# Token mixing steps drawn from one queue in a fused attention, mixture and gated-convolution kernel

## The chip, the cores and the metric

The kernel runs on one core of one Trainium2 chip. The metric is the device time of one execution in microseconds (us), as the median of several runs. The core has five engines that matter here: PE (TensorE, matrix products), DVE (VectorE), ACT (ScalarE), POOL (GpSimd) and SP (SyncE, which issues the DMAs). Each works through its own list of instructions in order and waits for the others only through semaphores.

## What is computed

Batch 4, sequence 768, 8 heads of 48, so 384 channels. The reference, cut to what matters:

```python
# gated linear attention, per batch and head
state = alpha[t][:, None] * state + outer(k[t], v[t]);  x[t] = q[t] @ state
# mixture
theta = x @ w_theta
zr, zi = x * cos(theta), x * sin(theta)
y = w_tok_r @ zr + w_tok_i @ zi        # over the sequence: token mixing
u = x + y
x = u + relu(u @ w_ch)
# gated convolution
h = relu(x @ w_in);  out = (h * sigmoid(conv3(h, conv_w))) @ w_out
```

## The kernel before

The sequence of each batch is cut into six chunks of 128 rows. Chunks are numbered through: 0 to 5 are batch 0, 6 to 11 batch 1, 12 to 17 batch 2, 18 to 23 batch 3. All float32 products are made of three matmuls of split operands (`mm3`, L66: high by high, high by low, low by high), so a value is first split into a rounded high part (ACT, L72) and a rest (DVE, L73).

Three kinds of step are given in program order by the loops at L400 to L423:

- `a_att(b, c)` (L376): attention of one chunk. It loads the chunk after next, prepares the next one on DVE (`a_prep`: two scans L229 and L234 over the decays with a reciprocal L233 between, and a product L243 that scales q and k), makes the next chunk's scores on PE (`kps`, `sc`), and then computes the chunk's own `y` (scores by v, then q by the running state S), copies it to `x`, computes `kv` for the state, and transposes x (`xps`) into `u`. The new state is `tst` on DVE (L296, old S plus `kv`), then two products by the decay on POOL (L304).
- `a_theta(ci)` (L325): splits u (`zh`, L72 and L73), nine matmuls `th`, then sine and cosine on ACT with DVE between (L343 to L347, tile `zf`, two buffers), the product with x (L348), and the split into `zh` and `zl` (six buffers each). L344 on DVE is the last reader of the `th` bank.
- `m_mix(b, h, c)` (L355): token mixing, chunk c's share of half h (384 of 768 output rows) of batch b: 18 matmuls `yps` into three accumulators of the pool `ps_m`, which has three buffers. After the sixth chunk three DVE additions (L374) move them into `u`. Four batches, two halves and six chunks make 48 steps and 864 matmuls.

The token weights come as 64-bit words: `load_tok` loads a piece, DVE decodes it in three instructions (L115 to L117), and the returned function, called as `piece()` one step later, splits it into `wtok`. Six pieces belong to the first half, six to the second.

Before the change, batch 0's six attention steps run with its theta steps one behind and no mixing. Then, for each batch b, mixing of its first half goes with the attention of batch b + 1, and mixing of its second half with the theta steps of batch b + 1. The last batch is mixed behind the loop, where the weights of the later layers are loaded (L429 to L440): its first half at L441, its second half at L475 with the first channel products (`cps`) between. The rest (`hps` and `ops`, L580 on) follows.

PSUM has eight banks: three for `ps_m`, five for `ps_a`, which `kps`, `sc`, `y`, `kv`, `xps` and `th` share in turn. A tile of `ps_a` therefore waits until the fifth tile before it, in program order, has been read.

The program order is not the order on the engines. The framework schedules the instructions of each engine itself when the kernel is built (an instruction may pass earlier ones that are not ready by its own estimate of the times), so a matmul written later can stand earlier on PE.

Of the kernel before, what the change touches and what calls it, by code (L numbers as in the profile page):

```python
# [19 lines left out]
B, H, S, D = 4, 8, 768, 48  # L20
# [3 lines left out]
NC = S // P  # L24
# [20 lines left out]
def tile_gated_linear_attention__then__spectral_moe__then__conv_gate(  # L45
# [53 lines left out]
    def body(top, slow):  # L99
# [46 lines left out]
        with ExitStack() as ph1:  # L146
# [244 lines left out]
            if not slow:  # L391
                a_load(0)
                a_load(1)
                wps = ps_a.tile([P, 512], F32, tag="a", name="wps")
                ohf = onehot.rearrange("p a t -> p (a t)")
                for _ in range(NWARM):
                    nc.tensor.matmul(wps, ohf[:, :P], ohf[:, :512], start=True, stop=True)
                a_prep(0)
                a_score(0)
            for c in range(NC):  # L400
                a_att(0, c)
                if c == 0:
                    load_theta()
                else:
                    piece()
                piece = load_tok(0, c)
                if c > 0:
                    a_theta(c - 1)
            piece()
            a_theta(NC - 1)  # L410
            for b in range(B - 1):
                for c in range(NC):
                    m_mix(b, 0, c)
                    a_att(b + 1, c)
                    if b == 0:
                        if c > 0:
                            piece()
                        piece = load_tok(1, c)
                if b == 0:
                    piece()  # L420
                for c in range(NC):
                    m_mix(b, 1, c)
                    a_theta((b + 1) * NC + c)  # L423
            marks.clear()
            att_ctx.close()
            ps_n = top.enter_context(tc.tile_pool(name="ps_n", bufs=5, space=PSUM))
# [11 lines left out]
            cst = st_p.tile([P, 9 * 256], F32, tag="w", name="cst", bufs=STB)  # L438
            nc.sync.dma_start(out=cst[:, : 6 * NF].bitcast(U32), in_=conv_w.rearrange("p f k -> p (f k)").bitcast(U32))
            decode(cw.rearrange("p f k -> p (f k)"), cst, 3 * NF)  # L440
            for c in range(NC):  # L441
                m_mix(B - 1, 0, c)
            tok0_ctx.close()
            ux_p = top.enter_context(tc.tile_pool(name="ux", bufs=2, side="right"))

# [27 lines left out]
                xsp[b, h] = x2  # L473

            for c in range(NC):  # L475
                m_mix(B - 1, 1, c)
                if c == 1:
                    m_usplit(0, 0)
                    m_ch(0, 0, ps_n, "n")
                if c == 2:  # L480
                    m_usplit(0, 1)
                    m_ch(0, 1, ps_n, "n")
                if c == 3:
                    m_xsplit(0, 0)
# [211 lines left out]
```

## Time and profile before

| | |
|---|---|
| median of 3 runs | 580.08 us (578.15 to 581.35) |
| profiled execution | 579.94 us, of which the span from first to last instruction is 578.2 us |
| mean granted clock of TensorE | 0.978 of full speed |
| busy shares of the span | PE 96%, DVE 79%, ACT 59%, POOL 16% |
| token mixing matmuls `yps` | 864 of 4407 matmuls; 23% of the chain that ended last |
| DMA | 65.41 MB, 113 GB/s in the mean |

A busy share is a mean over the whole span; the stages differ. PE counts as busy while a matmul is in its pipeline, so a full PE can still run at half clock. Times within the profile count from the first instruction of the span.

### The profile page before, as it was taken

Reading aid. Unit: us, or ns where it says so; the run is one execution under the profiler, and the core shown is the slowest. Engines: PE = TensorE matmul, PEld = TensorE weight load, DVE = VectorE, ACT = ScalarE, POOL = GpSimd, SP = SyncE. Lnnn points to the kernel's source line nnn. Section 1 sums busy time; section 2 is a strip of 40 time slices with the busy share of each in tenths; the row PEclk is TensorE's granted clock in tenths of the full one; section 3 lists DMA queues with packets and bytes.
Section 4 is the critical chain, followed back from the end, with each engine's and each line's share of the span. In section 5 each row is a group of like instructions: output and inputs, shape, how many; then the busy total and the mean of one; then the engine's idle time right before and its main releaser. Section 6 shows DMA issues by size and latency. Waiting matters only on the chain.

```text
span 578.2 us, 10973 instructions
## 1 busy us (share of the span) xinstructions
PE 553.1 (96%) x4407; PEld 532.9 (92%) x4407; DVE 457.1 (79%) x688; ACT 338.4 (59%) x695; POOL 93.6 (16%) x99
## 2 busy tenths in 40 slices
PE   6878989989999999999999999999999999999995
PEld 3767879979999999999999999999999999999995
DVE  7899997899856676542658889997888889798780
ACT  3665655555864567542752345567776776667561
POOL 2447514341044400350000000000000000000000
PEclk9688998999999999999999999999999999999999
DMA  8454652564024500320014333401044544546001
GB/s 322 153 170 136 212 187 81 174 220 161 1 83 139 174 20 8 97 64 1 1 31 160 111 112 109 145 20 41 5 147 139 176 137 144 198 143 204 27 29 46
DMA packets 24986, 65.41 MB, mean 113 GB/s; under 512 B 2528, under 2 KB 8672, under 8 KB 24544
## 3 DMA queue, kind: packets, MB, share of 16 engines
q1 hardware_dynamic: 24928, 64.64, 33.9%
q8 instruction: 36, 0.59, 0.4%
q14 instruction: 22, 0.18, 0.1%
HBM read 59.92 MB, written 4.72 MB: 112 GB/s over the span
## 4 chain that ended last, share of the span: by engine, by line
PE 80%; DVE 3%; issue 1%; ACT 1%; ACTq 0%
PE yps L64 23%; PE hps L64 18%; PE ops L64 18%; PE cps L64 7%; PE th L64 5%; PE y L64 4%; PE sc L64 3%; PE kv L64 2%; PE xps L320 1%; PE kps L252 1%; DVE fbt L229 1%; DVE stage L116 1%; DVE fbt L234 0%; DVE wtok L73 0%; DVE stage L115 0%
## 5 line engine op out<-in xcount | busy, mean ns | idle before, releaser
L64 PE MATMUL yps<-wtok,zh 128*128 128x384 f32 x576 | 153.0, 343 | 0.0
L64 PEld LDWEIGHTS yps<-wtok,zh 128*128 128x128 f32 x576 | 105.2, 191 | 2.4 <-ACT pt L261 0.2
L64 PE MATMUL hps<-x,win 128*128 128x386 f32 x576 | 107.1, 339 | 0.0
L64 PE MATMUL ops<-wout,g 128*128 128x384 f32 x576 | 106.9, 338 | 0.0
L64 PEld LDWEIGHTS hps<-x,win 128*128 128x128 f32 x576 | 102.2, 189 | 0.0
L64 PEld LDWEIGHTS ops<-wout,g 128*128 128x128 f32 x576 | 101.7, 187 | 0.0
L64 PE MATMUL yps<-wtok,zl 128*128 128x384 f32 x288 | 96.9, 339 | 0.0
L262 POOL TENSOR_SCALAR_AFFINE_SELECT pt<-pt 128x512 f32<-128x512 f32 x48 | 53.8, 1142 | 147.6 <-ACT pt L261 147.6
L64 PEld LDWEIGHTS yps<-wtok,zl 128*128 128x128 f32 x288 | 54.4, 189 | 0.8
L521 ACT ACTIVATE cv<-cv 128x384 f32<-128x384 f32 x64 | 33.4, 523 | 32.1 <-DVE cv L518 32.1
L229 DVE TENSOR_TENSOR_SCAN fbt<-a_t,onehot 128x516 f32<-128x516 f32 x24 | 29.5, 1229 | 22.9 <-ACT a_t L240 21.2
L73 DVE TENSOR_TENSOR g<-cv,g 128x384 fp32r<-128x384 f32 x64 | 35.5, 555 | 14.8 <-ACT g L72 14.2
L64 PE MATMUL th<-wth,zh 128*128 128x384 f32 x216 | 44.0, 340 | 0.0
L515 DVE SCALAR_TENSOR_TENSOR cv<-hh,cw,cv 128x383 f32<-128x383 f32 (+1 forms) x64 | 38.3, 613 | 4.4 <-ACT cv L512 4.1
L522 DVE SCALAR_TENSOR_TENSOR cv<-cv,hh 128x384 f32<-128x384 f32 x64 | 35.2, 556 | 7.9 <-ACT cv L521 5.9
L512 ACT ACTIVATE cv<-hh,cw 128x384 f32<-128x384 f32 x64 | 38.3, 616 | 3.8 <-DVE g L73 3.3
L64 PE MATMUL cps<-us,wch 128*128 128x384 f32 x216 | 40.3, 339 | 0.0
L72 ACT CAST g<-cv 128x384 fp32r<-128x384 f32 x64 | 32.6, 509 | 11.6 <-DVE cv L522 10.1
L518 DVE SCALAR_TENSOR_TENSOR cv<-hh,cw,cv 128x384 f32<-128x384 f32 (+1 forms) x64 | 38.4, 614 | 0.7
L64 PEld LDWEIGHTS cps<-us,wch 128*128 128x128 f32 x216 | 38.0, 188 | 0.5 <-issue 0.3
L64 PEld LDWEIGHTS th<-wth,zh 128*128 128x128 f32 x216 | 37.4, 188 | 0.5 <-DVE zh L73 0.4
L64 PE MATMUL sc<-qk_t 48*128 48x128 f32 x384 | 34.3, 294 | 3.1 <-DVE tst L296 2.5
(84 smaller groups left out, 826.8 us busy)
## 6 DMA issues: line engine op xcount, KB each, us to landing
qk_t<-in_qka_dram SPq DMA_DIRECT2D x24, 512.0 KB, 4.6
stage<-in_w_tok_dram SPq DMA_DIRECT2D x12, 768.0 KB, 4.5
top<-in_w_tok_dram SPq DMA_DIRECT2D x12, 768.0 KB, 4.3
a_t<-in_qka_dram SPq DMA_DIRECT2D x24, 260.0 KB, 2.8
v_t<-in_v_dram SPq DMA_DIRECT2D x24, 192.0 KB, 3.9
out_dram<-ob SPq DMA_DIRECT2D x24, 192.0 KB, 1.9
stage<-in_w_in_dram SPq DMA_DIRECT2D x4, 768.0 KB, 5.8
stage<-in_w_out_dram SPq DMA_DIRECT2D x4, 768.0 KB, 4.4
```

Source lines behind the costliest of these rows:

```text
L64: nc.tensor.matmul(o, lhsT, rhs, start=start, stop=stop, skip_group_check=True)
L72: cast = nc.scalar.copy(hi, src)
L73: lo_eng.tensor_tensor(lo, src, hi.bitcast(F32), ALU.subtract)
L116: nc.vector.scalar_tensor_tensor(fb, hi, 0xC0000000, fb, ALU.bitwise_and, ALU.bitwise_or)
L229: nc.vector.tensor_tensor_scan(bf[:, AW:0:-1], at[:, AW:0:-1], of[:, AW:0:-1], 0.0, ALU.mult, ALU.add)
L252: nc.tensor.transpose(kps[:, p, :], kh[:, p, :], ident)
L262: nc.gpsimd.affine_select(pt, pt, [[0, NP], [1, P]], ALU.is_ge, 0.0, base=0, channel_multiplier=-1)
L512: nc.scalar.activation(cv, hh[:, o : o + HALF], AF.Copy, scale=cw[:, f, 1:2])
L515: nc.vector.scalar_tensor_tensor(cv[:, a:HALF], hh[:, o + a - 1 : o + HALF - 1], cw[:, f, 0:1], cv[:, a:HALF], ALU.mult, ALU.add)
L518: nc.vector.scalar_tensor_tensor(cv[:, 0:e], hh[:, o + 1 : o + 1 + e], cw[:, f, 2:3], cv[:, 0:e], ALU.mult, ALU.add)
L521: nc.scalar.activation(cv, cv, AF.Tanh, scale=0.5)
L522: nc.vector.scalar_tensor_tensor(cv, cv, 1.0, hh[:, o : o + HALF], ALU.add, ALU.mult)
```

## The change

The 48 mixing steps are put in one list (`mixes`), ordered by batch, half and chunk, and the loops take the next one with each step of attention or theta, from chunk 2 of batch 0 on. So batch 0's first half starts two chunks behind its theta steps, its last two shares go with the first two chunks of batch 1, and its second half follows at once. By the end of the loops 40 steps have been taken where it was 36; eight are left for the place behind the loop instead of twelve. The theta steps of batches 1 to 3 now go with the last two shares of the batch before and the first four shares of their own batch. `a_theta(5)`, the last of batch 0, moves behind the first attention step of batch 1, and the loads and splits of the second half's weights move one step.

```diff
--- before.py
+++ after.py
@@ -397,6 +397,7 @@
                     nc.tensor.matmul(wps, ohf[:, :P], ohf[:, :512], start=True, stop=True)
                 a_prep(0)
                 a_score(0)
+            mixes = [(b, h, c) for b in range(B) for h in range(2) for c in range(NC)]
             for c in range(NC):
                 a_att(0, c)
                 if c == 0:
@@ -404,23 +405,24 @@
                 else:
                     piece()
                 piece = load_tok(0, c)
+                if c > 1:
+                    m_mix(*mixes.pop(0))
                 if c > 0:
                     a_theta(c - 1)
-            piece()
-            a_theta(NC - 1)
-            for b in range(B - 1):
+            for b in range(1, B):
                 for c in range(NC):
-                    m_mix(b, 0, c)
-                    a_att(b + 1, c)
-                    if b == 0:
-                        if c > 0:
-                            piece()
+                    if b == 1:
+                        piece()
                         piece = load_tok(1, c)
-                if b == 0:
-                    piece()
+                    m_mix(*mixes.pop(0))
+                    a_att(b, c)
+                    if b == 1 and c == 0:
+                        a_theta(NC - 1)
                 for c in range(NC):
-                    m_mix(b, 1, c)
-                    a_theta((b + 1) * NC + c)
+                    if b == 1 and c == 0:
+                        piece()
+                    m_mix(*mixes.pop(0))
+                    a_theta(b * NC + c)
             marks.clear()
             att_ctx.close()
             ps_n = top.enter_context(tc.tile_pool(name="ps_n", bufs=5, space=PSUM))
@@ -438,8 +440,8 @@
             cst = st_p.tile([P, 9 * 256], F32, tag="w", name="cst", bufs=STB)
             nc.sync.dma_start(out=cst[:, : 6 * NF].bitcast(U32), in_=conv_w.rearrange("p f k -> p (f k)").bitcast(U32))
             decode(cw.rearrange("p f k -> p (f k)"), cst, 3 * NF)
-            for c in range(NC):
-                m_mix(B - 1, 0, c)
+            while mixes[0][1] == 0:
+                m_mix(*mixes.pop(0))
             tok0_ctx.close()
             ux_p = top.enter_context(tc.tile_pool(name="ux", bufs=2, side="right"))
 
@@ -473,7 +475,7 @@
                 xsp[b, h] = x2
 
             for c in range(NC):
-                m_mix(B - 1, 1, c)
+                m_mix(*mixes.pop(0))
                 if c == 1:
                     m_usplit(0, 0)
                     m_ch(0, 0, ps_n, "n")
```

What the engines' lists look like at the places that matter. In the names a number tells the tile apart; `wtok00` and `wtok01` are high and low part of the first half's weights, `wtok10` and `wtok11` of the second's.

PE, at `kv` of chunk 6, the first chunk of batch 1 (`x_920` and `x_974` are its x). Before:

```order
L64 MATMUL y_903<-v_t_620,pt_750 64x48 x2
L64 MATMUL y_903<-v_t_620,pt_753 64x48 x2
L64 MATMUL y_903<-v_t_620,pt_750 64x48 x2
L64 MATMUL y_903<-v_t_620,pt_753 64x48 x2
L64 MATMUL kv_922<-v_t_620,kt_756 64x96 x8
L64 MATMUL yps_845<-wtok00_84,zh_797 128x384
L64 MATMUL yps_845<-wtok01_85,zh_797 128x384
L64 MATMUL yps_846<-wtok00_84,zh_797 128x384
L64 MATMUL yps_846<-wtok01_85,zh_797 128x384
L64 MATMUL yps_847<-wtok00_84,zh_797 128x384
L64 MATMUL yps_847<-wtok01_85,zh_797 128x384
L320 MATMUL xps_936<-ident_73,x_920 128x128 x3
```

With the change:

```order
L64 MATMUL y_957<-v_t_659,pt_807 64x48 x2
L64 MATMUL y_957<-v_t_659,pt_810 64x48 x2
L64 MATMUL y_957<-v_t_659,pt_807 64x48 x2
L64 MATMUL y_957<-v_t_659,pt_810 64x48 x2
L64 MATMUL kv_976<-v_t_659,kt_813 64x96 x8
L320 MATMUL xps_990<-ident_73,x_974 128x128 x3
L64 MATMUL th_998<-wth0_115,zh_995 128x384
L64 MATMUL th_998<-wth1_116,zh_995 128x384
L64 MATMUL th_998<-wth0_115,zh_995 128x384 x2
L64 MATMUL th_998<-wth1_116,zh_995 128x384
L64 MATMUL th_998<-wth0_115,zh_995 128x384 x2
L64 MATMUL th_998<-wth1_116,zh_995 128x384
```

Six token matmuls stood between `kv` and the transposes; now the transposes follow at once, and behind them the nine matmuls of theta step 5 (`th_998`), which before (`th_825`) stood ahead of this chunk's `y`. The fifth `ps_a` tile before this `kv` was the `th` of theta step 5 and is now that of theta step 4. Counted over PE's list, 72 token matmuls stand ahead of the first `y` of batch 1 in both programs; ahead of the `y` of chunk 11, the last of batch 1, there are 156 before and 180 with the change. Between the last theta matmul and the first `cps` there are 126 before and 102 with the change.

DVE, around the `tst` behind `kv` of chunk 9, from which POOL makes the state for chunk 10. Before:

```order
L243 TENSOR_TENSOR qk_t_1180<-qk_t_1180,fbt_1291 128x1024
L296 TENSOR_TENSOR tst_1251<-S1_112,kv_1242 112x384
L115 TENSOR_SCALAR stage_1262<-stage_1262 128x768
L73 TENSOR_TENSOR zh_1487<-u_935,zh_1487 128x384
L116 SCALAR_TENSOR_TENSOR stage_1262<-stage_1262 128x768
L117 SCALAR_TENSOR_TENSOR stage_1262<-stage_1262 128x768
L73 TENSOR_TENSOR wtok11_87<-stage_1155,wtok10_86 128x2x384
L229 SCALAR_TENSOR_TENSOR fbt_1394<-a_t_1285,onehot_109 128x516
L233 RECIPROCAL starts_110<-fbt_1394 128x4
```

With the change:

```order
L116 SCALAR_TENSOR_TENSOR stage_1347<-stage_1347 128x768
L296 TENSOR_TENSOR tst_1336<-S1_112,kv_1327 112x384
L117 SCALAR_TENSOR_TENSOR stage_1347<-stage_1347 128x768
L73 TENSOR_TENSOR wtok11_87<-stage_1240,wtok10_86 128x2x384
L229 SCALAR_TENSOR_TENSOR fbt_1476<-a_t_1370,onehot_109 128x516
L73 TENSOR_TENSOR zh_1647<-u_989,zh_1647 128x384
L233 RECIPROCAL starts_110<-fbt_1476 128x4
L234 SCALAR_TENSOR_TENSOR fbt_1476<-a_t_1370,starts_110 128x516
L243 TENSOR_TENSOR qk_t_1372<-qk_t_1372,fbt_1476 128x1024
```

Before, the one-input decode step L115 stands behind `tst`; now L117, the split of a token weight piece and the next scan do, and `zh` comes behind the scan. From the start of DVE's list to the L243 for the scores of chunk 12, the changed list has one more L115, L116, L117 and `wtok` split and two more `zh` splits, and nothing less.

PE in the theta steps of batch 2 (chunks 12 to 17; `th_2403` is that of chunk 14 before, `th_2481` with the change). Before:

```order
L64 MATMUL yps_2299<-wtok11_87,zh_1610 128x384
L64 MATMUL yps_2299<-wtok10_86,zl_1630 128x384
L64 MATMUL th_2403<-wth0_115,zh_2400 128x384
L64 MATMUL th_2403<-wth1_116,zh_2400 128x384
L64 MATMUL yps_2297<-wtok10_86,zh_1651 128x384
L64 MATMUL yps_2297<-wtok11_87,zh_1651 128x384
L64 MATMUL yps_2297<-wtok10_86,zl_1671 128x384
L64 MATMUL yps_2297<-wtok10_86,zh_1651 128x384
L64 MATMUL yps_2297<-wtok11_87,zh_1651 128x384
L64 MATMUL th_2403<-wth0_115,zh_2400 128x384 x2
L64 MATMUL th_2403<-wth1_116,zh_2400 128x384
```

With the change:

```order
L64 MATMUL th_2437<-wth0_115,zh_2434 128x384
L64 MATMUL th_2481<-wth0_115,zh_2478 128x384
L64 MATMUL th_2481<-wth1_116,zh_2478 128x384
L64 MATMUL th_2481<-wth0_115,zh_2478 128x384 x2
L64 MATMUL th_2481<-wth1_116,zh_2478 128x384
L64 MATMUL th_2481<-wth0_115,zh_2478 128x384 x2
L64 MATMUL th_2481<-wth1_116,zh_2478 128x384
L64 MATMUL th_2481<-wth0_115,zh_2478 128x384
L64 MATMUL th_2522<-wth0_115,zh_2519 128x384
```

Before, each theta step is surrounded by mixing of the batch before, which waits for nothing new. Now the last 14 matmuls of that mixing stand between the first and the second theta step, the steps 13 to 17 follow one another (45 matmuls), and behind them comes mixing of batch 2 itself, which reads what these theta steps make. In batch 1 steps 9 to 11 still have mixing between them; in batch 3 the sixth step is spread over the mixing behind the fifth.

## Rows read from the trace of the kernel before

**Rows 1.** busy time by stretch; columns: stretch, length, PE, PEld, DVE, ACT, POOL, clock, DMA share, GB/s

```profile
47.41:127.50 80.09, 74.49 (x817) 68.04 (x817) 74.75 (x90) 49.68 (x102) 34.60 (x30) 0.94 0.53 173
...
127.50:300.80 173.30, 173.30 (x1706) 167.03 (x1705) 113.21 (x145) 101.23 (x205) 38.08 (x45) 1.00 0.20 64
...
300.80:578.20 277.40, 271.34 (x1541) 270.31 (x1539) 226.51 (x404) 162.15 (x339) 0.12 (x1) 1.00 0.33 111
```

**Rows 2.** waits of PE, 30 to 130 us; columns: total, times, longest

```profile
PE y L64 <- POOL S L304: 3.7, 2, 2.6
...
PE kv L64 <- DVE zf L344: 2.6, 1, 2.6
```

**Rows 3.** timeline of PE; columns: start us, us, engine, line, operation, shapes, count, wait

```profile
86.21 1.55 PE L64 MATMUL kv<-v_t,kt 128*64 128x96 f32 x16 [2.63 <-DVE zf L344]
...
127.50 1.14 PE L64 MATMUL y<-v_t,pt 128*64 128x48 f32 x32
...
301.02 0.51 PE L64 MATMUL yps<-wtok,zh 128*128 128x384 f32 x2
...
301.54 0.51 PE L64 MATMUL yps<-wtok,zh 128*128 128x384 f32 x2
```

**Rows 4.** waits of DVE, 90 to 110 us

```profile
DVE u L374 <- PE yps L64: 1.5, 2, 1.0
...
DVE wtok L73 <- ACT wtok L72: 1.4, 1, 1.4
...
DVE tst L296 <- PE kv L64: 1.3, 1, 1.3
```

**Rows 5.** timeline of DVE, batches 0 and 1

```profile
67.42 1.22 DVE L229 TENSOR_TENSOR_SCAN fbt<-a_t,onehot 128x516 f32<-128x516 f32 x1
...
81.70 0.53 DVE L344 SCALAR_TENSOR_TENSOR zf<-zf,th 128x384 f32<-128x384 f32 x1
...
109.07 0.61 DVE L115 TENSOR_SCALAR stage<-stage 128x768 uint32<-128x768 uint32 x1
...
109.72 1.15 DVE L116 SCALAR_TENSOR_TENSOR stage<-stage 128x768 uint32<-128x768 uint32 x1
...
110.90 0.96 DVE L117 SCALAR_TENSOR_TENSOR stage<-stage 128x768 uint32<-128x768 uint32 x1
...
111.78 0.95 DVE L73 TENSOR_TENSOR wtok<-stage,wtok 128x768 fp32r<-128x768 f32 x1
...
117.71 0.86 DVE L73 TENSOR_TENSOR zh<-u,zh 128x384 fp32r<-128x384 f32 x1
```

**Rows 6.** timeline of POOL, the updates of S

```profile
64.11 5.62 POOL L304 TENSOR_TENSOR S<-tst,ftot 48x192 f32<-48x192 f32 x2 [1.36 <-DVE tst L296]
...
108.76 1.29 POOL L304 TENSOR_TENSOR S<-tst,ftot 48x192 f32<-48x192 f32 x2
```

**Rows 7.** timeline of DVE, product L243 in batch 2 and weight split after the loops

```profile
168.02 1.47 DVE L243 TENSOR_TENSOR qk_t<-qk_t,fbt 128x1024 f32<-128x1024 f32 x1
...
308.71 1.42 DVE L73 TENSOR_TENSOR wch<-stage,wch 128x768 fp32r<-128x768 f32 x2
```

**Rows 8.** timeline of PE, next scores in batch 2 and first channel matmuls

```profile
170.77 0.60 PE L252 MATMUL kps<-ident,qk_t 128*128 128x128 f32 x4
...
318.52 4.91 PE L64 MATMUL cps<-us,wch 128*128 128x384 f32 x27
```

**Rows 9.** timeline of PE, first theta matmuls of batch 2

```profile
200.44 0.51 PE L64 MATMUL th<-wth,zh 128*128 128x384 f32 x2
```

**Rows 10.** timeline of ACT, theta step in batch 2

```profile
208.39 0.58 ACT L343 ACTIVATE zf<-th,magic 128x384 f32<-128x384 f32 x1
```

**Rows 11.** timeline of DVE, theta steps in batch 2

```profile
208.52 0.96 DVE L73 TENSOR_TENSOR zl<-zf,zh 128x768 fp32r<-128x768 f32 x1 [0.43 <-ACT zh L72]
...
213.73 0.96 DVE L73 TENSOR_TENSOR zl<-zf,zh 128x768 fp32r<-128x768 f32 x1 [0.27 <-ACT zh L72]
...
231.31 0.96 DVE L73 TENSOR_TENSOR zl<-zf,zh 128x768 fp32r<-128x768 f32 x1 [1.52 <-ACT zh L72]
```

## Prediction, made before the changed kernel was run

> **What bounds the kernel now.** I read the busy time by stretch first [rows 1]. From 127.50 us on, PE is busy for the whole 173.30 us up to 300.80 and for 271.34 of the 277.40 us after it, at a granted clock of 1.00 (the 2.4 GHz level). There is nothing to fill in there: only a matmul taken out of this part shortens it. A token matmul costs 0.173 us in it: three of them lie between the starts 301.02 and 301.54 [rows 3]. The front, 47.41 to 127.50 us (attention and theta of batches 0 and 1), is different: PE 74.49, DVE 74.75 of 80.09 us, ACT and POOL far less. So the question is whether the front can take in more matmuls without getting longer. The waits of PE tell who holds it there: `y` on POOL's S 3.7 us, `kv` on DVE's L344 2.6 us [rows 2]. Those of DVE, 90 to 110 us, come to 1.5 + 1.4 + 1.3 = 4.2 us [rows 4], the idle time that could be used on the engine which paces this stage. As marker for the end of the front I take `y` of chunk 11, at 127.50 us [rows 3].
>
> **What moves.** By the order of PE's list, 72 token matmuls stand ahead of batch 1's first `y` in both programs, so the early start in batch 0 gives almost nothing by itself: before, the scheduler already pulled them there. Ahead of the marker stand 156 before and 180 after. Behind it all 864 − 156 = 708 are 684 now: 24 × 0.173 = **−4.15 us**, if the marker stays where it is.
>
> **What holds the marker.** (1) DVE. Up to L243 for chunk 12 the new list has one decoded and split weight piece more, 0.61 + 1.15 + 0.96 + 0.95 = 3.67 us (109.07 to 111.78), and two `zh` splits, 2 × 0.86 (117.71): 5.4 us [rows 5]. The idle 4.2 us [rows 4] can take most of it. A DVE that runs without a gap makes the marker 5.4 − 4.2 = **+1.2 us** later; bounds 0, if DVE also uses its gaps before 90 us, and 5.4, if it uses none. I take 1.2, since the three waits are for work that the new order has earlier.
>
> (2) S for chunk 10. POOL's two products took 1.29 us at 108.76 and 5.62 us at 64.11 [rows 6]. In the first case DVE had L115 next, at 109.07, with one tensor input; in the second it had instructions that read two tensors, the last of them the scan from 67.42 to 68.64 [rows 5], and POOL ended 1.1 us behind that (69.73). In the new list `tst` behind chunk 9 is followed by L117, the weight split and the scan, which all read two tensors, where it was followed by L115. The product could thus last between 1.29 and 5.62 us. The `y` of chunk 10 needs it; of the extra 4.3 us, PE has some 1.6 to cover (nine theta matmuls, at 0.173). So 0 to 2.7 us; I take **+1.5**, nearest the row of 64.11, because in this stage a gap of DVE in front of the scan (it waits for ACT) lets POOL in about 1 us sooner.
>
> The Trainium skill speaks against the change at this point: its page "SBUF — State Buffer", section "Who interferes with whom", says that a DVE instruction with two inputs in SBUF and a GpSimd instruction that reads SBUF take the port one at a time, each holding it for its whole length, and that the issue order decides. The rows agree, with 5.62 us against 1.29 [rows 6]; by the rule alone every `tst` followed by two-input work would lose the whole 4.3 us, and 2.7 of it would reach PE.
>
> (3) The wait of `kv` in chunk 6, 2.63 us at 86.21 [rows 3], should go: its PSUM bank was read last by the L344 of theta step 5, and is now read last by that of step 4, which stood at 81.70 [rows 5], 4.5 us before this `kv` started. It is worth nothing by itself: PE has slack against DVE in this stage, and DVE arrives when it arrives. The same slack covers the accumulators of the second half, which wait for three additions L374 at the change of halves.
>
> (4) Cost nothing: the splits `zh` that now stand in the attention stages of batches 2 and 3 delay L243 by at most 0.86 us; it ended at 168.02 + 1.47 = 169.49 us [rows 7], the matmul that reads it started at 170.77 [rows 8], 1.3 us to spare. Behind the loops 24 matmuls fewer lie ahead of the first `cps` (102, not 126), 4.2 us less cover; the last weight split ended at 308.71 + 1.42 = 310.13 us [rows 7] and `cps` started at 318.52 [rows 8]: 8.4 us to spare, 4.2 left. Loads keep their number and size; one `w_tok` load moves one place on SP, and no wait of DVE above was for a load. POOL gets no new work.
>
> (5) The theta steps of batch 2 now follow one another, 45 matmuls in a row, and mixing of the same batch reads what they make. One chain, from ACT's L343 at 208.39 [rows 10] to the end of `zl` at 213.73 + 0.96 = 214.69 [rows 11], takes 6.3 us. With two `zf` buffers that is one `z` per 3.15 us; a mixing step takes 18 × 0.173 = 3.11 us. The first `z` of the batch was there 208.52 + 0.96 − 200.44 = 9.0 us after its theta step started [rows 9, 11], and PE has six theta steps of nine matmuls and 14 matmuls of old mixing ahead of the mixing that reads it: 68 × 0.173 = 11.8 us. So there are 2.8 us in hand against a loss of 0.04 per step: costs **0**.
>
> Sum: −4.15 + 1.2 + 1.5 = −1.45 us. Against the profiled execution's 579.94 us that is **578.5 us**; the median of the runs, 580.08, is 0.14 above it.
>
> **Rivals.** *A: nothing holds the marker.* DVE takes the additional 5.4 us into gaps, and S is early enough, because the new order gives PE its `kv` and transposes of chunk 6 at once, without the 2.63 us wait, and everything behind starts earlier. Then the whole 4.15 us is won: 575.8 us. For it: DVE's idle time in the front is 80.09 − 74.75 = 5.3 us [rows 1], about the additional work. Against: idle time of several small waits is hardly ever all used.
>
> *B: the list does what the loops say.* Eight steps behind the loop, not twelve, would be 4 × 3.11 = 12.4 us won: 567.5. Against it are the counts: of these 72 matmuls only 24 change their side of the marker, since the scheduler had taken the others early already.
>
> *C: the theta steps wait on each other, slower.* Place: the mixing of batches 1 to 3 behind their own theta steps. Before, five `zl` took from 208.52 to 231.31, 4.56 us each [rows 11], with mixing of the old batch between. If the chain goes at that pace when bunched too, the sixth `z` comes 9.0 + 5 × 4.56 = 31.8 us in, and PE, with 11.8 + 5 × 3.11 = 27.4 us of work ahead of that step's mixing, waits 4.4 us, less what it can take of the next attention (some 1.5, the scores and `y` of a chunk, 1.14 of it the `y` [rows 3]): 2.9 in batch 2, 2.9 in batch 3 and about half, 1.5, in batch 1, where steps 9 to 11 still have mixing between: 7.3 us, so 578.5 + 7.3 = 585.8. It decides from (27.4 + 1.5 − 9.0)/5 = 4.0 us per `z` on. Against it: the 4.56 us were PE's own pace, since it had nine theta and 18 mixing matmuls per step, 27 × 0.173 = 4.67; the chain by itself takes 3.15.
>
> **How the numbers follow.** A measurement of this kernel can tell about 0.5%, or 2.9 us, from no change. The forecast's case, with costs (1) and (2) between 0.5 and 5 us together, lies from 576.3 to 581 and has 0.59, chiefly within 0.5%. A has 0.28, at or below 576, B 0.02: together 0.30 faster. C, and the upper ends of (1) and (2) together, which would be −4.15 + 5.4 + 2.7 = +3.95, 583.9, have 0.11 slower. The range leaves out B, the largest part of C and the sum of the upper ends: 575.0 (A, and 0.8 more from a DVE that is earlier) to 582.5.
>
> **What would show it.** Right: the `kv` wait on L344 in chunk 6 is gone; the `y` of chunk 11 starts at 127.5 + 2.7 = 130.2 us, with DVE busy for over 95% of the stage ahead; POOL's S behind chunk 9 takes over 3 us; from the marker to the end the time is 4.15 us shorter, PE waiting for nothing. Case A: the marker at 127.5 or before. Wrong: PE waits for ACT's `zh` or DVE's `zl` in the theta stages (C, if these waits pass 3 us together); a wait of `cps` on `wch`; a granted clock below 1.00 behind the marker; a marker behind 133.

## The result, and the profile after

The changed kernel is slower. Its median is 585.43 us (584.09 to 586.97, 6 runs), that of the kernel before on the same chip 579.86 us: a ratio of 1.0095 (95% interval 1.0074 to 1.0117), or 5.5 us (4.3 to 6.8) more. Forecast were 578.5 us, with a range of 575.0 to 582.5. The profiled execution has a span of 584.3 us (578.2 before); mean granted clock 0.981; PE is busy for 95% of the span, DVE for 78%, ACT for 58%, POOL for 16%.

The busy time by stretch of the changed kernel, cut at the `y` of chunks 7, 11, 12, 17 and 18 (columns as in [rows 1]: stretch, length, PE, PEld, DVE, ACT, POOL, clock, DMA share, GB/s):

```profile
47.41:96.59 49.18, 41.35 (x430) 36.86 (x428) 48.87 (x58) 31.61 (x65) 18.30 (x16) 0.97 0.52 163
...
96.59:133.00 36.41, 36.16 (x435) 32.36 (x434) 30.75 (x39) 19.28 (x39) 16.55 (x16) 1.00 0.58 185
...
133.00:170.90 37.90, 37.04 (x253) 35.11 (x252) 28.45 (x37) 23.33 (x45) 2.96 (x2) 1.00 0.16 50
...
207.79:244.95 37.16, 37.16 (x254) 34.92 (x252) 24.42 (x32) 21.59 (x42) 2.96 (x2) 1.00 0.15 49
```

The last three stretches of the kernel before, between the same matmuls:

```profile
95.85:127.50 31.65, 29.77 (x414) 27.37 (x413) 26.95 (x33) 17.66 (x37) 13.43 (x16) 1.00 0.59 193
...
127.50:157.49 29.99, 29.99 (x221) 28.64 (x219) 28.53 (x37) 19.50 (x39) 2.96 (x3) 1.00 0.26 87
...
193.75:227.97 34.22, 34.22 (x249) 33.75 (x247) 25.16 (x33) 21.86 (x45) 2.64 (x2) 1.00 0.16 53
```

From the `y` of chunk 7 to that of chunk 11 the changed kernel takes 36.41 us instead of 31.65, from there to the `y` of chunk 12 37.90 instead of 29.99, and in the theta stage of batch 2 37.16 instead of 34.22. Part of that is work that moved in. In the first of these stretches stand 90 token matmuls instead of 68, by their starts (one more still runs at its beginning). The token matmuls alone, before and after (busy time by stretch of the tile `yps`: stretch, length, PE, PEld, DVE, clock, DMA share, GB/s):

```profile
95.85:127.50 31.65, 13.44 (x68) 11.64 (x68) 1.66 (x3) 1.00 0.59 193
```

```profile
96.59:133.00 36.41, 18.69 (x91) 15.16 (x90) 1.60 (x3) 1.00 0.58 185
```

Ahead of the `y` of chunk 7 DVE is full (48.87 of 49.18 us); behind it PE is busy nearly throughout, so what it is busy with has to be read from its timeline. At chunk 8 (timeline of PE; columns as in [rows 3]):

```profile
100.08 1.16 PE L64 MATMUL sc<-qk_t 48*128 48x128 f32 x8
...
101.16 1.32 PE L64 MATMUL yps<-wtok,zh 128*128 128x384 f32 x6
...
102.41 1.16 PE L64 MATMUL sc<-qk_t 48*128 48x128 f32 x8
...
103.50 0.55 PE L64 MATMUL y<-v_t,pt 128*64 128x48 f32 x10
...
106.26 0.79 PE L64 MATMUL y<-v_t,pt 128*64 128x48 f32 x20
...
133.00 1.14 PE L64 MATMUL y<-v_t,pt 128*64 128x48 f32 x32
```

The scores, one block of 16 matmuls in the source, stand in two pieces of eight with six token matmuls between, and `y` in several pieces too. Such a place, where token matmuls stand inside a block, is called a cut below. In the theta stage of batch 2, at the scores for chunk 18, first the changed kernel, then the kernel before:

```profile
228.96 0.38 PE L252 MATMUL kps<-ident,qk_t 128*128 128x128 f32 x2
...
229.27 0.48 PE L64 MATMUL sc<-qk_t 48*128 48x128 f32 x2
...
229.68 1.34 PE L64 MATMUL yps<-wtok,zh 128*128 128x384 f32 x6
...
233.03 0.49 PE L64 MATMUL sc<-qk_t 48*128 48x128 f32 x4
...
236.81 0.49 PE L64 MATMUL sc<-qk_t 48*128 48x128 f32 x4
...
240.58 0.49 PE L64 MATMUL sc<-qk_t 48*128 48x128 f32 x4
...
242.25 0.48 PE L64 MATMUL sc<-qk_t 48*128 48x128 f32 x2
...
244.95 1.14 PE L64 MATMUL y<-v_t,pt 128*64 128x48 f32 x32
```

```profile
226.87 1.16 PE L64 MATMUL sc<-qk_t 48*128 48x128 f32 x16
...
227.97 1.14 PE L64 MATMUL y<-v_t,pt 128*64 128x48 f32 x32
```

Five pieces up to the `y` at 244.95, most with a whole mixing step between (a piece, then 18 token matmuls), and `kps` in two, where one block of 16 stood. The five pieces take 0.41 + 0.42 + 0.42 + 0.42 + 0.41 = 2.08 us to the starts behind them, the block 227.97 − 226.87 = 1.10.

To add this up I took PE's timeline row by row, from each row's start to the next one's, and put it down to the kind of matmul. From the `y` of chunk 7 to the first `cps` (95.85 to 318.52 us before, 96.59 to 325.21 after):

| us | before | after | difference |
|---|---|---|---|
| scores `sc` | 16.38 | 19.44 | +3.06 |
| `y` and `kv` | 37.56 | 38.82 | +1.26 |
| token matmuls `yps` (5 more by PE's list: +0.87) | 126.56 | 130.47 | +3.91 |
| `xps`, `kps`, `th` | 40.29 | 39.03 | −1.26 |
| waits | 1.88 | 0.86 | −1.02 |
| together | 222.67 | 228.62 | +5.95 |

The same scores, `y` and `kv` cost 4.3 us more, and the token matmuls 3.0 us more than their number says. Ahead of this stretch the changed kernel is 0.74 us later (its first `y` already 1.2 us, before anything that the change touches), behind it 0.59 us shorter: 5.95 + 0.74 − 0.59 = 6.1 us, the difference of the spans.

The waits of PE, 127 us to the end (columns as in [rows 2]):

```profile
PE yps L64 <- DVE wtok L73: 0.9, 1, 0.9
```

And from 30 to 97 us:

```profile
PE yps L64 <- ACT zh L72: 5.7, 3, 2.2
...
PE sc L64 <- DVE tst L296: 3.9, 1, 3.9
...
PE xps L320 <- ACT x L286: 2.4, 2, 2.1
```

The waits of [rows 2] on POOL's S and on L344 are gone, and others stand in their place. Nothing behind 127 us waits for a `z`.

### The profile page after: what moved, and what is told of

The parts are those of the page before. It is cut to its first block, busy times and chain, and to the rows that moved or that the text cites. A ratio compares the mean times of both kernels' runs of the same rounds, so it can differ in the third digit from the quotient of the medians.

```text
span 584.3 us, 10994 instructions
## 1 busy us (share of the span) xinstructions
PE 556.3 (95%) x4407; PEld 532.0 (91%) x4407; DVE 455.2 (78%) x688; ACT 337.2 (58%) x695; POOL 93.4 (16%) x99
## 4 chain that ended last, share of the span: by engine, by line
PE 82%; ACT 1%; DMA 1%; DVE 1%; issue 0%; ACTq 0%; SPq 0%
PE yps L64 24%; PE hps L64 17%; PE ops L64 17%; PE cps L64 7%; PE th L64 5%; PE y L64 4%; PE sc L64 3%; PE kv L64 1%; PE xps L320 1%; DMA stage<-in_w_tok_dram 1%; PE kps L252 1%; ACT pt L261 0%; ACT a_t L240 0%; DVE stage L116 0%; DVE wtok L73 0%
## 5 line engine op out<-in xcount | busy, mean ns | idle before, releaser
L64 PE MATMUL yps<-wtok,zh 128*128 128x384 f32 x576 | 147.4, 343 | 6.5 <-ACT zh L72 5.7
L64 PEld LDWEIGHTS yps<-wtok,zh 128*128 128x128 f32 x576 | 102.0, 188 | 10.6 <-ACT zh L72 6.2
L64 PE MATMUL yps<-wtok,zl 128*128 128x384 f32 x288 | 91.0, 338 | 0.0
L73 DVE TENSOR_TENSOR g<-cv,g 128x384 fp32r<-128x384 f32 x64 | 35.6, 556 | 14.8 <-ACT g L72 13.1
L64 PE MATMUL th<-wth,zh 128*128 128x384 f32 x216 | 42.6, 348 | 0.0
L64 PE MATMUL sc<-qk_t 48*128 48x128 f32 x384 | 38.7, 301 | 3.9 <-DVE tst L296 3.9
L64 PEld LDWEIGHTS sc<-qk_t 48*128 48x128 f32 x384 | 30.9, 196 | 12.1 <-issue 6.8
L514 ACT ACTIVATE cv<-hh,cw 128x384 f32<-128x384 f32 x64 | 37.1, 615 | 2.7 <-DVE g L73 2.6
```

The costliest lines, as they stand in the source:

```text
L64: nc.tensor.matmul(o, lhsT, rhs, start=start, stop=stop, skip_group_check=True)
L73: lo_eng.tensor_tensor(lo, src, hi.bitcast(F32), ALU.subtract)
L514: nc.scalar.activation(cv, hh[:, o : o + HALF], AF.Copy, scale=cw[:, f, 1:2])
```

## The experiments

All times are medians; a ratio is that to the kernel before, run between on the same chip.

**1. Undo the pieces in the theta stages.** The next batch's first scores are issued behind the theta loop:

```diff
-                    a_score(ci + 1)
+                    if slow or (ci + 1) % NC or ci + 1 == NC:
+                        a_score(ci + 1)
...
                     a_theta(b * NC + c)
+                if b < B - 1 and not slow:
+                    a_score((b + 1) * NC)
```

> The changed kernel, but the first scores of the next batch are issued behind the theta loop, not ahead of it; on PE they then stand in one piece in batch 2 (in the changed kernel in five pieces between mixing steps) and in two pieces in batch 1 (in four). Theory P (PE pays for blocks of small matmuls that are cut into pieces by token matmuls): of the 2.0 us lost in the theta stage of batch 2 and the 1.3 us in that of batch 1 some 2.5 us come back, 585.4 to about 583. Rival Z (the bunched theta steps deliver z too late): the chain is not touched, 585.4, no change. Rival F (the loss lies in the front alone): no change either.

Measured: 584.48 us, ratio 1.0089 (1.0065 to 1.0113): less came back than expected, and the interval overlaps that of the change. The trace tells both halves. The scores for chunk 18 are whole again:

```profile
235.79 1.16 PE L64 MATMUL sc<-qk_t 48*128 48x128 f32 x16
```

and from the `y` of chunk 13 to that of chunk 19 the run takes 72.2 us instead of 74.0. In batch 1 0.8 us come back likewise, but a wait for a `wtok` split grows from 0.86 to 1.73 us. In the trace 1.8 us are left of it up to the first `cps`, in the medians 0.3 to 0.9. The trace bears out the theory's price in batch 2; the times by themselves do not show it.

**2. The sixth theta step ahead of batch 1 again** (`a_theta(NC - 1)` back in front of the loop, all else as changed).

> The changed kernel, but the sixth theta step of batch 0 stays ahead of batch 1's first attention step, as in the kernel before. On PE the pieces stay nearly as they are (13 cuts of scores instead of 14), and 180 token matmuls stand ahead of the y of chunk 11 as with the change. Theory P: 585 within 1 us. Rival F (moving that theta step is what makes the front longer): 2 to 4 us come back, 581 to 583.

Measured: 583.64 us, 1.0070 (1.0049 to 1.0091), 1.4 us less than the change by the ratios: between the two theories. By this a quarter of the loss could be the moved step's, but the intervals overlap, so it is not told from nothing.

**3 and 4. A shorter head start.** The queue starts two, then three steps early (`if c > 3`, `if c > 2` instead of `if c > 1`), the sixth theta step ahead; in the second of them the scores also behind the theta loop.

> The queue starts at chunk 4 of batch 0 (two steps early, not four), and the sixth theta step of batch 0 stays ahead of batch 1's attention. On PE the scores are then cut in two places as in the kernel before, 160 token matmuls stand ahead of the y of chunk 11 (156 before), 117 between last theta and first cps (126 before). Theory P: 579.9 less 4 x 0.173 = 579.2, no slower than before. Rival Z: theta steps follow one another with 18 token matmuls between, half of the loss stays, 582 to 583.

> As the run with two early steps, but three, and the next batch's first scores issued behind the theta loop. Two cuts of scores as before, none in the theta stages; 162 token matmuls ahead of the y of chunk 11. Theory P: 579.9 less 6 x 0.173 = 578.8. Rival Z: the theta steps are bunched nearly as in the changed kernel, 583 to 585.

Measured: 579.21 us, 0.9999 (0.9980 to 1.0018), as expected; and 581.70 us, 1.0048 (1.0028 to 1.0068), 2.9 us more than expected. The first shows that the queue in this short form neither wins nor loses. In the second PE waits in batch 1 for POOL's S and masked scores (1.2 and 1.0 us), and 1.3 us for nothing that the profile shows; why three steps bring these and two don't was not followed further.

**5. The price of lost turns.** In the kernel before, the 16 score matmuls of 12 chunks go first all on rows 0 to 47, then all on rows 64 to 111:

```diff
-                for p in range(NP):
-                    for j in range(2):
+                for p, j in [(p, j) for p in range(NP) for j in range(2)] if slow or ci < 2 * NC else [(p, j) for j in range(2) for p in range(NP)]:
```

> The kernel before, but in batches 2 and 3 (12 chunks) the score matmuls are issued first all of one tile (rows 0 to 47 of PE), then all of the other (rows 64 to 111), not in turn. Nothing is cut. Theory P in its first part (a cut also breaks the turns, so that two score matmuls no longer run side by side): 8 of one tile took 1.16 us, 16 in turn took 1.16 too, from start to next start 2.2 against 1.09; 12 x 1.1 = 13 us, 579.5 to 592. Rival (only the change between kinds of matmul costs): no change, 579.5.

Measured: 586.23 us, 1.0096 (1.0068 to 1.0124), 5.6 us, half of what was expected. Timeline of PE, the scores for chunk 14 and what follows:

```profile
172.96 1.71 PE L64 MATMUL sc<-qk_t 48*128 48x128 f32 x16
...
174.60 1.14 PE L64 MATMUL y<-v_t,pt 128*64 128x48 f32 x32
```

A block without turns takes 174.60 − 172.96 = 1.64 us, in turns 1.10: 12 × 0.54 = 6.5 us. All twelve blocks show it. So the turns matter, at half the price that I had read from two blocks of eight with something between them. The Trainium skill, "TensorE: Matmul & The Clock Gate", section "Packing small matmuls — row/col tiling", says that matmuls on different row groups run at the same time in the array; the trace agrees, with 1.10 against 1.64 us for the same 16.

**6. 24 token matmuls out of the front.** The changed kernel; two mixing steps between the `y` of chunks 8 and 9 compute only the product of the high parts:

```diff
+                        if not slow and (b, h, c) in [(0, 1, 0), (0, 1, 1)]:
+                            mm(mixps[d][:, :HALF], zz[0][:, i, ds_], wtok[h][0][:, i, c, :], c == 0 and i == 0, False)
+                            continue
                         mm3(
```

> The changed kernel without 24 of its token matmuls: the two steps for chunks 0 and 1 of batch 0's second half compute only the product of the high parts. All 24 stood between the y of chunk 8 and that of chunk 9. Theory P (from the y of chunk 7, 96 us, on PE sets the time): 24 x 0.173 = 4.2 us less, and one cut of kv and the length of two others gone, 585.4 to about 580.5. Rival D (the prediction's: DVE sets the time until the y of chunk 11): the matmuls are hidden there, 585.4, no change.

Measured: 585.36 us, 1.0084 (1.0056 to 1.0112). Theory P falls as the whole cause: the 4.2 us on PE are worth some 0.6 (the intervals overlap). PE does reach the `y` of chunk 9 earlier (18.4 us behind that of chunk 7, 21.3 with the change), and then this happens (POOL, PE, and busy time by stretch):

```profile
112.33 5.52 POOL L304 TENSOR_TENSOR S<-tst,ftot 48x192 f32<-48x192 f32 x2 [1.98 <-DVE tst L296]
```

```profile
114.29 1.14 PE L64 MATMUL y<-v_t,pt 128*64 128x48 f32 x32
...
117.91 1.55 PE L64 MATMUL y<-S,qk_t 128*64 128x96 f32 x16 [2.48 <-POOL S L304]
```

```profile
117.00:126.00 9.00, 8.09 (x57) 7.59 (x59) 5.47 (x6) 2.78 (x7) 3.38 (x5) 0.63 0.57 168
```

POOL's S takes 5.52 us, PE waits 2.48 us for it, and behind the wait the granted clock is 0.63 in the mean, most of it at the lower level (1.2 GHz). The next `y` starts 12.5 us later, not 7.2. This is the prediction's term (2), with its very size (0 to 2.7 us reaching PE); in the changed kernel itself it does not appear, since PE is late there and POOL finds DVE idle. The profiled execution is the slowest of this run's ten, 588.06 us, 2.7 us over their median: how much of this wait the others had is not shown.

**7. The price of a cut.** In the kernel before, six token matmuls are wedged into the middle of the 16 scores of 10 chunks, the turns kept:

```diff
+                        if (p, j) == (2, 0) and wedge:
+                            behind(m, ("mix",))
+                        marks["sc"] = m
+                    if p == 1:
+                        wedge = held.pop(ci, None)
...
+                                for m in mm3(*a):
+                                    behind(m, ("sc",))
+                                    marks["mix"] = m
```

> The kernel before, but in 10 chunks of batches 2 and 3 six of the token matmuls that would stand elsewhere are wedged into the middle of the 16 score matmuls, with the turns between the two tiles kept. No matmul more or less. Theory P in its second part (the change between the kinds costs by itself): about 0.1 us at each of the two borders, 10 x 0.2 = 2 us, 579.5 to 581.5, at most 10 x 0.4 = 4 us. Rival: a cut is free, 579.5.

Measured: 584.92 us, 1.0073 (1.0044 to 1.0101), 4.2 us. One such place in PE's timeline:

```profile
165.98 0.72 PE L64 MATMUL sc<-qk_t 48*128 48x128 f32 x8
...
166.63 0.62 PE L64 MATMUL yps<-wtok,zh 128*128 128x384 f32 x2
...
167.88 0.71 PE L64 MATMUL sc<-qk_t 48*128 48x128 f32 x8
...
168.52 1.14 PE L64 MATMUL y<-v_t,pt 128*64 128x48 f32 x32
```

The two halves take 0.65 + 0.64 = 1.29 us (whole 1.10), the six token matmuls between them 1.25 (6 × 0.173 = 1.04): 0.40 us per cut, 4.0 for ten. All ten cut blocks take 1.29 or 1.30 us. So a cut costs by itself, half of it in the scores and half in the token matmuls.

**8. Nearly all cuts undone at once.** The queue with its four early steps stays. Experiments 1 and 2 together, and the mixing step is issued behind the theta step in batch 0 and behind the attention step in batch 1, and batch 0's mixing is kept behind the scores and `kv`:

```diff
-                    m_mix(*mixes.pop(0))
-                    a_att(b, c)
+                    if b == 1:
+                        a_att(b, c)
+                        m_mix(*mixes.pop(0))
...
+                            if not slow and (b, h) <= (0, 1):
+                                behind(m, ("sc", "kv"))
```

> The changed kernel with nearly all cuts undone at once: the next batch's first scores behind the theta loop, batch 0's sixth theta step ahead of batch 1, mixing issued behind the attention step in batches 0 and 1 and kept behind its scores and kv. The queue itself, its four early steps, and the bunched theta steps stay; 162 token matmuls stand ahead of the y of chunk 11 (180 with the change, 156 before), and 5 cuts of scores are left in the front up to 96 us, where PE has idle time, and one behind. Theory P: all but about 1 us of the loss goes, 579.5 to 580.5. Rivals Z (bunched theta steps) and E (the early start itself): 583 to 585.

Measured: 582.85 us, 1.0036 (1.0012 to 1.0061): 3.4 us of the 5.5 are gone, 2.1 (0.7 to 3.5) are left. Both forecasts missed, theory P's 579.5 to 580.5 by more. The bunched theta steps are all still there, and PE waits for nothing behind 140 us, which speaks against rival Z. Rival E is not settled: in this form 162 token matmuls stand ahead of the `y` of chunk 11, so 18 of the 24 early ones have fallen back behind it, and the 3.4 us are not the cuts' alone. Runs 13 to 16 come back to this.

**9 to 12. S on DVE.** In the kernel before and in the runs 6, 8 and 3, L304 goes to DVE:

```diff
-                        nc.gpsimd.tensor_tensor(
+                        nc.vector.tensor_tensor(
                             Sn[r, :, j * D : (j + 1) * D],
```

> The kernel before with the two products that make the new state S on DVE instead of POOL. In the front of the kernel before, y waited 3.7 us for POOL's S, all of it ahead of 70 us. Theory S (POOL's product is held up while DVE works, and y waits for it): these waits go, DVE gets two short products per chunk more; 577 to 578.5 against 579.3 to 580.7 of the kernel before. Rival D (DVE sets the time of the front up to 96 us): the waits turn into others, 579.5 to 581.

> The changed kernel without the same 24 token matmuls as in the run with 24 less, and S on DVE. That run won 3.6 us up to the y of chunk 9 and lost it by that of chunk 10: POOL's S took 5.5 us, PE waited 2.5 us for it and its clock was lower behind the wait. Theory S: with S on DVE that is not given back, 24 x 0.173 less: 581 to 582.5, where the run with POOL's S had 585.4. Rival D (DVE's row of work itself is as long): 584 to 586.

> The run with nearly all cuts undone, and S on DVE. That run had 582.85 us, with waits of y for S (1.7 us) and for POOL's masked scores (1.0 us) in batch 1. Theory S: the first go, and the clock behind them comes back: 580 to 581.5. Rival D: 583.

> The run with two early steps (579.2 us, as long as the kernel before), and S on DVE; 163 token matmuls stand ahead of the y of chunk 11 (160 without it, 156 before). Theory S: 577 to 578.5, faster than both kernels. Rival D: 579 to 580.5, no gain.

| run | us | ratio | without S on DVE |
|---|---|---|---|
| 9, kernel before | 583.22 | 1.0031 (1.0008 to 1.0053) | 1 |
| 10, 24 less | 586.54 | 1.0093 (1.0059 to 1.0126) | 1.0084 |
| 11, all whole | 585.11 | 1.0080 (1.0052 to 1.0108) | 1.0036 |
| 12, two early | 582.07 | 1.0030 (1.0010 to 1.0051) | 0.9999 |

Theory S falls four times: the waits for S go, and no kernel gets faster. The kernel before loses 0.3%, clear of its interval; runs 11 and 12 lose by their ratios, with intervals that overlap those of runs 8 and 3; run 10 does not move. All four lie above rival D's values. In run 10 DVE's row itself is too long; why the other three lose was not followed further. Busy time of run 10:

```profile
96.00:134.00 38.00, 35.28 (x432) 30.65 (x431) 37.37 (x52) 21.50 (x44) 10.65 (x8) 1.00 0.61 182
```

37.37 of 38.00 us on DVE, the fifth column. (In run 10 PE's 24 matmuls are out as well, and it gains nothing.)

**13 to 16. Less work for DVE.** L116 and L117 are left out for the six weight pieces of the second half (their weights are decoded in part), in the kernel before and in the change, run 8 and run 6:

```diff
             nc.vector.tensor_scalar(fb, hi, 3, 0x3FFFFFFF, ALU.logical_shift_left, ALU.bitwise_and)
+            if short and not slow:
+                return
```

> The kernel before without L116 and L117 for the six weight pieces of the second half (their weights are then decoded in part): 6 x 2.1 = 12.7 us less for DVE, nearly all of it between 90 and 133 us. Control. Theory DP (in the kernel before PE alone sets the time behind 96 us, DVE ends a little sooner): only the 1.9 us of PE's waits between 115 and 126 us can go, 578 to 580 against 580. Rival D (DVE sets it): 3 us or more less, 577 or below.

> The changed kernel without L116 and L117 for the same pieces. On PE the pieces of y and kv at chunk 8 are whole, those of the scores in the theta stages stay. Theory DP (with the change DVE and PE are about equally long between 96 and 133 us): PE's own row is what remains, with its pieces of y and kv gone; 2 to 3 us less, 582.5 to 583.5. Rival D (DVE alone): 5 us less or more, 580.5. Rival PE alone: 584.5 to 585.5.

> The run with nearly all cuts undone (582.85), without the same DVE work. Theory DP: both causes are gone, and the queue's order by itself costs nothing: as the control within 1 us, 578.5 to 580. Rival Z (the bunched theta steps cost by themselves): 582 to 583.

> The changed kernel without the 24 token matmuls and without the same DVE work. Theory DP: now that DVE is out of the way the 24 matmuls are worth their 4.2 us, 4 us less than the changed kernel with the short decoding: 578.5 to 579.5. Rival (PE never sets the time there): as that run, 582.5 to 583.5.

| run | us | ratio | with the whole decoding |
|---|---|---|---|
| 13, kernel before | 575.47 | 0.9905 (0.9876 to 0.9934) | 1 |
| 14, the change | 582.22 | 1.0031 (1.0002 to 1.0060) | 1.0095 |
| 15, all whole | 575.50 | 0.9917 (0.9891 to 0.9943) | 1.0036 |
| 16, 24 less | 578.80 | 0.9987 (0.9951 to 1.0022) | 1.0084 |

The control missed its theory: 5.5 us won, not two. So taking work from DVE shortens the front of the kernel before too; timeline of PE in run 13, the `y` of chunks 7 and 11:

```profile
93.54 1.14 PE L64 MATMUL y<-v_t,pt 128*64 128x48 f32 x32
...
122.48 1.14 PE L64 MATMUL y<-v_t,pt 128*64 128x48 f32 x32
```

They come 2.3 and 5.0 us earlier than before. Four things follow; all figures are from the ratios. Against its own control the form with the cuts undone is now equal (0.9917 to 0.9905): the queue's order and the bunched theta steps cost nothing by themselves, with 6 of the 24 early matmuls. The change with its cuts is 1.3% behind the control, 7.3 us. The 24 matmuls, worth 0.6 us beside the full DVE, are worth 2.6 (1.0031 to 0.9987, intervals that overlap) once DVE is out of the way. And run 16, which has 24 matmuls fewer than the control and none more ahead of the `y` of chunk 11 (156 as before), is still 4.8 us slower (0.9987 to 0.9905, intervals apart). Its scores are still cut. Busy time of the scores by stretch, from the `y` of chunk 7 to the first `cps`, run 13 and run 16 (stretch, length, PE, PEld, ACT, clock, DMA share, GB/s):

```profile
93.54:312.89 219.35, 17.50 (x241) 14.56 (x240) 17.10 (x32) 1.00 0.29 92
```

```profile
94.46:316.53 222.07, 21.03 (x240) 16.43 (x240) 17.13 (x32) 1.00 0.25 81
```

The same 240 matmuls keep PE busy for 21.0 us instead of 17.5; counted from start to start as in the table above, scores cost 3.0 us more and token matmuls 3.2 more than their number says. So rival E cannot be the whole of it: the cuts cost without the early matmuls and without DVE's load. What the sixth theta step's place (run 2) adds to run 16 is not separated. The front of the changed kernel has two bounds of nearly the same length: PE's 24 matmuls alone are worth 0.6 us, DVE's work alone 3.7, both together 6.3.

**17 and 18. The same room, with nothing left out.** The low part (L73) of those six pieces goes to POOL, in the kernel before and in run 8:

```diff
-                cast = split(out_hi, out_lo, full, nc.vector)
+                cast = split(out_hi, out_lo, full, nc.gpsimd if second and not slow else nc.vector)
```

> The kernel before, with the low part (L73) of the six second-half weight pieces subtracted on POOL instead of DVE: 6 x 0.95 = 5.7 us less for DVE in the front, and six long instructions more for POOL, which is busy for 35 of 80 us there. The run without L116 and L117 showed that 12.7 us less on DVE are worth 5.5 us in this kernel. Theory DP: 5.7/12.7 of that, 2.5 us, 578 where the kernel before has 580.5; with the low part later by some us for the matmuls that need it, 579. Rival (POOL's and DVE's two-input work hold each other up): 580.5 to 583.

> The run with nearly all cuts undone (2.1 us over the kernel before), with the same low parts on POOL. Its shortened form won 6.9 us. Theory DP: 3 us less, 579.5 to 580. Rival: 583 and above.

Measured: 585.63 us, 1.0095 (1.0069 to 1.0122), and 587.34 us, 1.0130 (1.0100 to 1.0161): slower, as the rival says, run 17 beyond its 583. POOL's L73 and DVE's L117 beside it in run 17:

```profile
111.79 2.41 POOL L73 TENSOR_TENSOR wtok<-stage,wtok 128x768 fp32r<-128x768 f32 x1
```

```profile
112.56 2.46 DVE L117 SCALAR_TENSOR_TENSOR stage<-stage 128x768 uint32<-128x768 uint32 x1
```

L117 takes 2.46 us instead of the 0.96 of [rows 5]: it started at 112.56, while POOL's subtraction ran from 111.79 to 114.20, and ended 0.8 us behind it. The 0.95 us taken from DVE come back as 1.5. Four of the six pieces show it. PE waits for no late low part in run 17. Here the hold-up of [rows 6] runs the other way: POOL started first and DVE was kept waiting. The Trainium skill, "SBUF — State Buffer", section "Who interferes with whom", says that the issue order decides which of the two is blocked; the trace agrees, with 2.46 us for 0.96.

No version that does the whole work beat the kernel before by more than the measurement can tell; the one with two early steps equals it.

## Why the prediction was wrong

The forecast case (−1.45 us) and its range fell. Two steps failed: (5), which put the bunched theta steps at 0, where the cuts that came with them cost 3.7 us by the trace; and the sum as a whole, which has no term for the 24 matmuls' own time on PE ahead of the marker. The time that rival C gave, 585.8 us, is close to the 585.43 measured, but by chance: its mechanism is not there. L344, one per theta step, in batch 2 of the changed kernel (timeline of DVE):

```profile
225.57 0.55 DVE L344 SCALAR_TENSOR_TENSOR zf<-zf,th 128x384 f32<-128x384 f32 x1
...
228.92 0.55 DVE L344 SCALAR_TENSOR_TENSOR zf<-zf,th 128x384 f32<-128x384 f32 x1
...
232.27 0.55 DVE L344 SCALAR_TENSOR_TENSOR zf<-zf,th 128x384 f32<-128x384 f32 x1
```

One `z` per 3.35 us, near the 3.15 worked out and far from the 4.0 from which C decides, and no wait of PE for a `z`.

- **What moves** (24 matmuls, −4.15 us): the number was right, the 24 crossed the marker. What failed is the sentence ahead of it, "only a matmul taken out of this part shortens it": a matmul has no fixed price. I counted token matmuls in PE's list and did not look at what they stand between. The list of the changed program shows the pieces as plainly as the counts.
- **The front's room on PE**, a term put at nothing: that PE "has slack against DVE in this stage" goes back to [rows 1], one mean over 80 us. Of PE's 5.6 us without work there (80.09 − 74.49) two thirds lay ahead of the `y` of chunk 7. Behind it, where 22 more token matmuls landed, PE had waited for 1.88 of 31.65 us. The stretch grew by 4.8 us: 3.8 for the 22 matmuls and 2.7 for pieces (scores 1.1, `y` and `kv` 1.0, token matmuls 0.6), less 1.6 of waits. PE is not the only bound there: run 6, with the 24 taken out, won 0.6 us, run 16, with DVE relieved as well, 2.6.
- **Step (5), "costs 0"**: this is the step that failed most. The chain of `z` was weighed and was harmless. Not weighed was what PE does while the theta steps follow one another: the next batch's scores stand in pieces between mixing steps, 2.0 us in the theta stage of batch 2 (scores 0.98, token matmuls about 1.07 beyond their number), 1.7 in that of batch 1. Runs 5 and 7 measured both parts of the price, run 1 gave back 1.9 us in batch 2 of its trace, and run 8 3.4 us in all, part of it perhaps by the 18 matmuls that fell back. Why the scheduler cuts them is argued only: a score tile needs a bank of `ps_a`, and the bunched theta steps hold all five until their L344.
- **(1), DVE, +1.2 us**: the additional 5.4 us are right, and that DVE paces the front as well (run 13). It was busy for 30.75 of the 36.41 us ahead of the marker, 84% where over 95% was forecast. Wrong was that its gaps would take 4.2 of them. L243 for chunk 12 stood at 124.28 in the kernel before and stands at 129.22 now, of which 1.2 us are the later start of this execution. Timeline of DVE, before and after:

```profile
124.28 1.47 DVE L243 TENSOR_TENSOR qk_t<-qk_t,fbt 128x1024 f32<-128x1024 f32 x1
```

```profile
113.00 0.55 DVE L296 TENSOR_TENSOR tst<-S,kv 112x384 f32<-112x384 f32 x1
...
115.79 0.96 DVE L73 TENSOR_TENSOR wtok<-stage,wtok 128x768 fp32r<-128x768 f32 x1 [2.24 <-ACT wtok L72]
...
116.85 1.23 DVE L229 TENSOR_TENSOR_SCAN fbt<-a_t,onehot 128x516 f32<-128x516 f32 x1
...
129.22 1.47 DVE L243 TENSOR_TENSOR qk_t<-qk_t,fbt 128x1024 f32<-128x1024 f32 x1
```

Between the `y` of chunks 7 and 11 DVE is idle for 36.41 − 30.75 = 5.7 us now, 31.65 − 26.95 = 4.7 before. The old waits are gone, new ones have come (waits of DVE, 30 to 160 us):

```profile
DVE wtok L73 <- ACT wtok L72: 2.5, 2, 2.2
...
DVE stage L115 <- DMA stage<-in_w_tok_dram: 2.5, 3, 1.4
```

It waits for the loads of the weight pieces, for which it had no wait before, and longer for ACT's casts. So I had an upper bound of 5.4 in hand and took a value near the lower one: gaps were counted as if any work could fill them. By the ratios 1.4 us of the loss would be DVE's (run 8 loses 2.1 us, in its short form 0.7), with intervals too wide to tell it from nothing.
- **(2), S, +1.5 us**: 0 here. POOL's S behind chunk 9 took 1.08 us:

```profile
113.63 1.08 POOL L304 TENSOR_TENSOR S<-tst,ftot 48x192 f32<-48x192 f32 x2 [3.63 <-DVE tst L296]
```

because DVE, with the order that I had read, stood idle from 113.55 to 115.79 waiting for ACT, and POOL used that. The mechanism was right and appears as soon as PE is early (run 6).
- **(3)** held: the wait on L344 is gone, and from the `y` of chunk 6 to that of chunk 7 it took 13.6 us, before 13.4: nothing won. **(4)** held for the splits `zh` and for `cps`, which wait for nothing; the mixing behind the marker now waits 0.86 us for a weight split, which was not on the list.
- The marker at 133.00 us, 5.5 us later (forecast 2.7, "wrong behind 133"), was the right place to look. From it to the end the changed kernel takes 451.3 us, before 450.7: the −4.15 are eaten by the pieces in two theta stages (3.7) and the wait (0.86).

## To carry to other kernels

When work moves within an engine's list, read the rows around the places where it lands, not only the counts: small matmuls that ran in turns on different rows cost half as much again when they lose their turns, and each cut by wide matmuls cost 0.4 us here. A stage's mean hides where in it an engine is idle: look at the stretch in which the work lands. Where two engines are equally long in a stage, neither shows its full worth in a single experiment; take work from each and from both. And idle time between dependent steps is no room for new work unless that work is ready just then.

## What the runs showed of the hardware

Two things I had not expected, with their numbers. Sixteen score matmuls on 48 rows each take 1.10 us in turns between rows 0 to 47 and 64 to 111, and 1.64 us one group after the other. And a token matmul next to one of them on PE costs about 0.1 us more on either side of the border (0.40 us per cut with two new borders, run 7), with no wait in the profile: PE counts as busy throughout.
